# Windowed attention into a mixture of attention experts: the experts' outputs turned by DMA transposes, and some masks and casts moved to GpSimd

## The chip, the cores and the metric

The kernel runs on one core of a Trainium2 chip. The core has TensorE (PE in the profile; PEld is its weight load), VectorE (DVE), ScalarE (ACT), GpSimd (POOL) and SyncE (SP). All loads and stores are issued by SP and carried by 16 DMA engines. The metric is the time of one execution on the device in microseconds, as the median of several runs; the profile shows one such execution, from its first to its last instruction (its span).

## The reference

There are two parts. The first is attention with a sliding window over q, k and v of shape 8 batches x 8 heads x 576 rows x 64, where a row sees the rows at most 32 away. Its output, with the heads side by side, is x: 8 x 576 x 512. The second part has four attention experts over x, and a gate that picks two experts for each row:

```python
scores = np.where(np.abs(pos[:, None] - pos[None, :]) <= 32, scale * q @ k.T, -1e9)
x = softmax(scores) @ v                       # heads side by side: 8 x 576 x 512
logits = x @ w_gate                           # the two best of 4 experts, softmax of the two
for e in range(4):
    a = softmax(causal(scale * (x @ wq[e]) @ (x @ wk[e]).T))   # 576 x 576, head size 64
    out += weight_of_e_for_the_row * (a @ (x @ wv[e]) @ wo[e])
```

Inputs and outputs are float32. The kernel computes the window part with float32 matmuls and the experts with bf16 matmuls.

## The kernel before, in words

The work is cut into named steps, and a long string, `ORDER` (L22), lists them in the order in which they are emitted. Each engine executes its own instructions in that order; engines meet through semaphores. The string's entries carry the PSUM slots that a step uses after a colon: there are four slots of two banks, `P0` to `P3`, and each step that needs PSUM names its own. The `step` calls from L533 on hold the durations and dependencies that were used to lay out the order; at run time only the string matters.

The window part works on 16 groups i of four heads (two groups g per batch b):

- `load.i.qn` and `load.i.kn` (L117) bring q and k in rows as they lie in memory, 0.59 MB each; `natp` holds three buffers for each, so a load waits for the turn three groups earlier. The first two groups (`LONG`) use larger pieces.
- `turn.i.*` (L272) transposes them in blocks of 32x32 on VectorE: 2 or 6 instructions.
- `S.i.half` (L285) makes scores of 128 keys against 192 or 256 queries on TensorE, the exponential on ScalarE (three pieces for each pair of heads), and the multiplication with the band mask (L306). `MASKS` (L62) says which engine multiplies: VectorE for the groups 0 and 1, GpSimd for the other 14.
- `U.i.x` and `E.b` (`win_av` and `win_av_end`, L326 and L337) multiply with v, which `loadv.b` loads (1.18 MB) and `dup.b.n` doubles for odd blocks, on ScalarE and GpSimd; VectorE divides by the sum and writes `XN`.
- `T.b.g` and `TE.b` turn `XN` on TensorE, ScalarE copies it to `XTF` (float32) and GpSimd casts it to `XTB` (bf16).

The expert part works on batches b and pairs j of experts:

- `WL.q/v/o` load the weights and `WC.q/v/o` (L250) cast them to bf16 on ScalarE.
- `G1.b`, `G3.b`: gate. `QK.b.j.n`, `V.b.p`: projections. `PS.b.j.c`: causal scores, exponential on ScalarE, mask on GpSimd.
- `AV.b.j` (L469) multiplies with the values; VectorE scales the result by the gate's weight over the sum and writes `OE` (bf16, rows on partitions, 64 columns for each of two experts). There is one `OE` for each j, so batch b+1 overwrites that of batch b.
- `PT.b.j` (L489) turns `OE`: five TensorE transposes of 128x128 into a PSUM slot, and one VectorE copy into `OTT` (two buffers, by the parity of b).
- `Y.b.t` (L497) multiplies `OTT` with the output weights, ScalarE copies the result out of PSUM and SP stores it.

Steps `w<n>` (L216) run n matmuls on zeros to keep TensorE active while it has nothing to do, and `late.0` sets constants. SP's instructions, loads, stores and all, are one queue in program order; each transfer also waits for the one eight places before it.

Of the kernel before, what the change touches and what calls it, by code (L numbers as in the profile page):

```python
# [9 lines left out]
BF16 = mybir.dt.bfloat16  # L10
# [12 lines left out]
    load.0.qn load.0.kn load.1.kn turn.0.qn turn.0.kn load.1.qn turn.1.kn turn.1.qn loadv.0 w18:2 S.0.0:01  # L23
    w12:2 S.1.0:10 load.2.qn S.0.1:23 dup.0.0 dup.0.2 WL.q load.2.kn dup.0.3 turn.2.qn dup.0.1 S.1.1:20
    load.3.qn load.3.kn w5:1 U.1.0:3 U.0.0:2 U.1.1:0 U.0.1:3 E.0:2 turn.2.kn WC.q late.0 T.0.1:0 T.0.0:3
    turn.3.qn TE.0:2 turn.3.kn S.2.0:01 QK.0.0.0:2 WL.v S.3.0:03 QK.0.0.1:2 G1.0:1 WC.v S.2.1:20 G3.0
    QK.0.1.0:3 loadv.1 dup.1.0 V.0.0:2 dup.1.2 dup.1.3 QK.0.1.1:1 load.4.kn dup.1.1 PS.0.0.0:3 S.3.1:02
    turn.4.kn load.4.qn V.0.1:3 PS.0.0.1:1 load.5.kn turn.4.qn PS.0.1.0:0 U.3.0:3 load.6.qn U.2.0:2
    PS.0.0.2:1 S.4.0:03 load.5.qn turn.5.kn E.1:1 WL.o U.2.1:2 load.7.kn U.3.1:0 loadv.2 PS.0.0.3:1
    turn.5.qn PS.0.1.1:3 TE.1:2 T.1.0:1 T.1.1:0 PS.0.1.2:2 S.4.1:31 AV.0.0:0 QK.1.0.0:2 WC.o V.1.0:3  # L30
    PS.0.1.3:2 S.5.0:01 turn.6.qn AV.0.1:3 QK.1.1.0:2 QK.1.0.1:0 load.6.kn dup.2.1 PT.0.0:3 dup.2.0
    QK.1.1.1:2 load.8.kn PS.1.0.0:0 loadv.3 dup.2.3 S.5.1:31 dup.2.2 turn.6.kn V.1.1:2 G1.1:0 load.8.qn
    PS.1.0.1:2 G3.1 S.6.0:13 U.4.0:2 U.5.1:0 PS.1.0.2:2 load.9.qn load.7.qn dup.3.2 PS.1.1.0:1 E.2:3 U.4.1:0
    S.6.1:32 PT.0.1:0 U.5.0:1 PS.1.0.3:0 PS.1.1.1:3 load.9.kn Y.0.0:2 TE.2:1 T.2.0:0 T.2.1:3 turn.7.kn
    turn.7.qn dup.3.0 AV.1.0:1 loadv.4 turn.8.qn dup.3.1 S.7.0:02 turn.8.kn PS.1.1.2:3 V.2.0:1 QK.2.0.0:0
    Y.0.2:2 dup.3.3 PT.1.0:3 S.7.1:01 S.8.0:23 QK.2.0.1:0 G1.2:1 PS.1.1.3:0 PS.2.0.0:2 dup.4.0 U.7.1:3
    U.6.1:0 G3.2 dup.4.1 E.3:2 QK.2.1.0:3 PS.2.0.1:0 V.2.1:1 Y.0.4:2 QK.2.1.1:3 PS.2.0.2:0 load.10.kn
    turn.9.kn S.8.1:21 dup.4.3 load.10.qn U.6.0:3 U.7.0:0 PS.2.0.3:1 PS.2.1.0:2 T.3.0:3 turn.9.qn AV.1.1:0
    turn.10.kn PS.2.1.1:2 load.11.kn TE.3:1 T.3.1:3 turn.10.qn PS.2.1.2:2 load.12.qn S.9.0:01 PT.1.1:2
    dup.4.2 V.3.0:3 Y.1.0:2 AV.2.0:1 PS.2.1.3:3 QK.3.0.0:0 load.11.qn loadv.5 S.9.1:32 S.10.0:01 load.12.kn  # L40
    V.3.1:3 AV.2.1:2 Y.1.2:3 QK.3.0.1:0 PT.2.0:1 turn.11.kn turn.11.qn QK.3.1.0:2 PS.3.0.0:0 S.10.1:13
    QK.3.1.1:2 dup.5.1 PS.3.0.1:0 load.13.qn G1.3:1 PS.3.1.0:2 PS.3.0.2:0 U.9.0:3 G3.3 U.8.0:2 U.8.1:0 E.4:1
    dup.5.2 U.9.1:3 dup.5.0 PS.3.0.3:0 PS.3.1.1:2 TE.4:1 Y.1.4:0 T.4.0:3 T.4.1:1 turn.12.qn turn.12.kn
    dup.5.3 S.11.0:02 S.12.0:13 AV.3.0:0 loadv.6 QK.4.0.0:2 load.13.kn V.4.0:1 load.14.qn PS.3.1.2:2
    S.11.1:30 QK.4.0.1:1 dup.6.0 PT.2.1:2 load.15.qn G1.4:3 PS.3.1.3:2 PS.4.0.0:1 Y.2.0:0 V.4.1:2 G3.4
    turn.13.kn dup.6.1 QK.4.1.0:1 load.14.kn S.12.1:02 E.5:1 U.11.1:3 PS.4.0.1:0 QK.4.1.1:1 AV.3.1:3
    PS.4.0.2:0 PS.4.1.0:1 U.10.0:2 U.10.1:0 U.11.0:1 loadv.7 PS.4.1.1:2 PS.4.0.3:0 T.5.0:3 turn.13.qn
    PT.3.0:1 turn.14.kn TE.5:2 T.5.1:0 PS.4.1.2:3 S.13.0:21 PT.3.1:0 Y.2.2:3 turn.14.qn V.5.0:0 QK.5.0.0:1
    dup.6.3 AV.4.0:3 PS.4.1.3:0 S.13.1:12 dup.7.2 QK.5.1.0:0 QK.5.0.1:3 V.5.1:2 AV.4.1:1 dup.6.2 Y.2.4:3
    dup.7.0 QK.5.1.1:2 PS.5.0.0:0 dup.7.3 E.6:3 load.15.kn U.12.0:1 PS.5.0.1:0 PS.5.1.0:3 U.13.0:2 G1.5:1  # L50
    PS.5.0.2:2 PS.5.1.1:3 U.12.1:0 G3.5 U.13.1:2 PS.5.1.2:3 turn.15.qn T.6.0:0 Y.3.0:1 PT.4.0:3 TE.6:2
    T.6.1:0 PT.4.1:3 Y.3.2:2 PS.5.0.3:3 turn.15.kn S.14.0:10 S.15.0:32 G1.6:1 V.6.0:0 Y.3.4:2 G3.6 dup.7.1
    QK.6.0.0:3 AV.5.0:2 PS.5.1.3:1 S.15.1:30 QK.6.0.1:1 V.6.1:2 QK.6.1.0:3 PS.6.0.0:1 S.14.1:20 QK.6.1.1:3
    AV.5.1:1 PS.6.0.1:2 PS.6.1.0:3 U.15.1:0 U.14.1:2 PS.6.0.2:3 PS.6.1.1:0 E.7:1 U.15.0:2 U.14.0:1
    PS.6.1.2:0 PS.6.0.3:2 T.7.1:3 T.7.0:1 TE.7:2 PT.5.0:0 Y.4.0:3 PT.5.1:0 PS.6.1.3:1 G1.7:2 AV.6.0:1
    QK.7.0.0:3 Y.4.2:0 QK.7.0.1:3 G3.7 QK.7.1.0:1 Y.4.4:0 PS.7.0.0:3 Y.5.0:2 QK.7.1.1:0 PS.7.0.1:3 AV.6.1:1
    PS.7.1.0:0 PS.7.0.2:3 V.7.0:2 PS.7.1.1:1 Y.5.2:3 PT.6.0:0 PS.7.0.3:1 PS.7.1.2:2 V.7.1:0 PT.6.1:1 Y.5.4:3
    AV.7.0:0 PS.7.1.3:3 Y.6.0:1 AV.7.1:0 PT.7.0:3 Y.6.2:1 PT.7.1:3 Y.6.4:1 Y.7.0:3 Y.7.2:1 Y.7.4:3
# [3 lines left out]
MASKS = ["DVE"] * 2 + ["POOL"] * 14  # L62

LONG = range(2)
DUP = ["ACT", "POOL", "ACT", "POOL"]

S = 576
# [6 lines left out]
def kernel(  # L74
# [12 lines left out]
    nc = tc.nc  # L87
# [162 lines left out]
    def cast_weights(n):  # L250
        if n == "q":
            for j in range(2):
                for m in range(2):
                    nc.scalar.copy(WQK[j][m], wtmp[j][:, m, :, :])
        else:
            nc.scalar.copy({"v": WV, "o": WO}[n], wtmp[n])
# [232 lines left out]
    def moe_turn(b, j):  # L489
        OE, OTT = OES[j], OTS[b % 2]  # L490
        pt = slot("pt", BF16)[:, 0, :]
        for qt in range(NQT):
            nc.tensor.transpose(pt[:, 128 * qt:128 * qt + 128], OE[:, qt, :, :].rearrange("p e d -> p (e d)"),  # L493
                                ident_bf)
        nc.vector.tensor_copy(OTT[:, j, 0:S], pt[:, 0:S])
# [37 lines left out]
    for b in range(B):  # L533
        for g in range(2):
            i = 2 * b + g
            for nm in ("kn", "qn"):
                step(("load", i, nm), lambda b=b, g=g, nm=nm: load(b, g, nm), 0,
                     [("turn", i - 3, nm)] if i > 2 else [],
                     [("SP", 1.35, -1), ("DMA", 1.95, 0), ("LAT", 0.8, 1)] if i in LONG else
                     [("SP", 1.8, -1), ("DMA", 2.3, 0), ("LAT", 0.8, 1)])  # L540
                step(("turn", i, nm), lambda b=b, g=g, nm=nm: turn(b, g, nm), 0,
                     [("load", i, nm)] + ([("S", i - 2, 1)] if i > 1 else []),
                     [("DVE", 2.45 if i in LONG else 1.6, -1)])
            for half in range(2):
                mk = ("DVE", (0.68, 0.55)[half]) if MASKS[i] == "DVE" else ("POOL", (1.35, 1.12)[half])
                step(("S", i, half), lambda b=b, g=g, half=half: win_scores(b, g, half), (1.75, 1.1)[half],
                     [("turn", i, nm) for nm in ("kn", "qn")] + ([("S", i, 0)] if half else []) +
                     ([("U", i - 3, 0), ("U", i - 3, 1), ("E", (i - 3) // 2)] if i > 2 else []),
                     [("ACT", (1.1, 0.8)[half], -1), (*mk, 0), ("ACT", (1.1, 0.8)[half], -1), (*mk, 2)], (0, 2))
            for x in range(2):  # L550
                step(("U", i, x), lambda b=b, g=g, x=x: win_av(b, g, x), 0.98,
                     [(("S", i, h), n) for h in range(x + 1) for n in (1, 3)] +
                     [("dup", b, n) for n in range(4)] +
                     ([("T", b - 1, g)] if b else []),
                     [("DVE", 0.75, -1)], (0,))
# [7 lines left out]
        for g in range(2):  # L563
            step(("T", b, g), lambda b=b, g=g: win_turn(b, g), 0.88,
                 [("U", 2 * b + g, x) for x in range(2)] + XT,
                 [("ACT", 0.48, -1), ("POOL", 0.6, 0), ("ACT", 0.48, -1), ("POOL", 0.6, 2)], (2,))
# [5 lines left out]
        for n in range(4):  # L572
            step(("dup", b, n), lambda b=b, n=n: double_v(b, n), 0, [("loadv", b)],
                 [(DUP[n], {"ACT": 0.9, "POOL": 1.25}[DUP[n]], -1)])
        X4 = [("T", b, 0), ("T", b, 1), ("TE", b)]
        XF = [(("T", b, g), n) for g in range(2) for n in (0, 2)] + [(("TE", b), 0)]
        if b == 0:
            step(("late", 0), late_constants, 0, [], [("ACT", 0.2, -1), ("POOL", 1.2, -1)])
        if b == 0:
            for n, us in (("q", 5.8), ("v", 3.1), ("o", 1.5)):  # L580
# [3 lines left out]
                     [("ACT", {"q": 2.2, "v": 0.9, "o": 0.9}[n], -1)])  # L584
# [4 lines left out]
        for j in range(2):  # L589
# [5 lines left out]
            for c in range(4):  # L595
                step(("PS", b, j, c), lambda b=b, j=j, c=c: moe_scores(b, j, c), (0.22, 0.25, 0.24, 0.06)[c],
# [7 lines left out]
            step(("PT", b, j), lambda b=b, j=j: moe_turn(b, j), 0.3,  # L604
                 [("AV", b, j)] + ([("Y", b - 2, t) for t in (0, 2, 4)] if b > 1 else []) +
                 ([("PT", b, 0)] if j else []) + ([("late", 0)] if b == 0 else []), [("DVE", 0.4, -1)], (0,))
        for p in range(2):
            step(("V", b, p), lambda b=b, p=p: moe_proj_v(b, p), (1.75, 0.44)[p],
# [55 lines left out]
```

## Time and profile before

The kernel takes 255.18 us, the median of 3 runs (254.45 to 255.73). The profiled execution took 254.34 us, with a span of 252.6 us and a mean granted TensorE clock of 0.993.

| Engine | busy us of 252.6 | share |
|---|---|---|
| PE | 236.0 | 93% |
| ACT | 190.5 | 75% |
| PEld | 183.5 | 73% |
| DVE | 167.6 | 66% |
| POOL | 147.2 | 58% |

The DMA engines moved 40.49 MB, at 160 GB/s on the mean. Busy times are averages over a span whose parts have different limits: the row of DMA shares and a table of busy time by stretches tell more than the totals. A group's row in the profile reads: line, engine, operation, written tile <- read tiles, shape, count | busy us, mean ns of one | idle time of the engine just before, and what ended it.

The work that the change touches:

| What | where | count | mean ns |
|---|---|---|---|
| transposes of OE | TensorE L493 | 80 | 219 |
| copies to OTT | VectorE L495 | 16 | 450 |
| masks of groups 0 and 1, half 0 / half 1 | VectorE L306 | 4 / 4 | 976 / 689 |
| masks of the other groups, half 0 / half 1 | GpSimd L306 | 28 / 28 | 1545 / 1277 |
| casts of q and k weights | ScalarE L254 | 4 | 617 to 620 |
| warm-up matmuls | TensorE L219 | 35 | 506 |

### The profile page before, as it was taken

Reading aid. Unit: us, or ns where it says so; the run is one execution under the profiler, and the core shown is the slowest. Engines: PE = TensorE matmul, PEld = TensorE weight load, DVE = VectorE, ACT = ScalarE, POOL = GpSimd, SP = SyncE. Lnnn points to the kernel's source line nnn. Section 1 sums busy time; section 2 is a strip of 40 time slices with the busy share of each in tenths; the row PEclk is TensorE's granted clock in tenths of the full one; section 3 lists DMA queues with packets and bytes.
Section 4 is the critical chain, followed back from the end, with each engine's and each line's share of the span. In section 5 each row is a group of like instructions: output and inputs, shape, how many; then the busy total and the mean of one; then the engine's idle time right before and its main releaser. Section 6 shows DMA issues by size and latency. Waiting matters only on the chain. (4 is left out here: it accounts for less than half of the span.)

```text
span 252.6 us, 9868 instructions
## 1 busy us (share of the span) xinstructions
PE 236.0 (93%) x4115; PEld 183.5 (73%) x4115; DVE 167.6 (66%) x480; ACT 190.5 (75%) x372; POOL 147.2 (58%) x200
## 2 busy tenths in 40 slices
PE   7787999899999989999999999999999999999982
PEld 2455867678878878788877877898777877976640
DVE  6968954785776693788388826896568364653552
ACT  2169579969789978789889689678878868657842
POOL 6033078849596769668577499359607677350410
PEclk9997999999999999999999999999999999999999
DMA  6999999999999993069599499655140310024247
GB/s 179 300 200 202 216 163 221 209 212 207 208 205 216 238 247 117 3 169 213 153 200 262 97 223 213 186 103 121 53 118 32 139 23 3 3 86 148 112 155 253
DMA packets 74780, 40.49 MB, mean 160 GB/s; under 512 B 46832, under 2 KB 69872, under 8 KB 74736
## 3 DMA queue, kind: packets, MB, share of 16 engines
q1 hardware_dynamic: 74736, 39.87, 70.6%
q8 instruction: 32, 0.52, 0.9%
q14 instruction: 12, 0.10, 0.2%
HBM read 30.42 MB, written 9.44 MB: 158 GB/s over the span
## 5 line engine op out<-in xcount | busy, mean ns | idle before, releaser
L306 POOL TENSOR_TENSOR AT<-AT,MASKP 128x640 f32<-128x640 f32 (+1 forms) x56 | 77.6, 1411 | 28.4 <-ACT AT L303 26.1
L303 ACT ACTIVATE AT<-sc 128x384 f32<-128x384 f32 (+4 forms) x192 | 70.5, 393 | 20.9 <-PE sc L296 19.2
L455 ACT ACTIVATE ATE<-ps 128x1024 bf16<-128x1024 f32 (+1 forms) x64 | 51.9, 834 | 13.5 <-PE ps L452 12.9
L296 PE MATMUL sc<-Tqn,KT 32*128 32x192 f32 (+1 forms) x1280 | 55.3, 314 | 5.9 <-ACT AT L303 2.8
L296 PEld LDWEIGHTS sc<-Tqn,KT 32*128 32x128 f32 x1280 | 48.0, 187 | 12.0 <-ACT AT L303 4.1
L459 POOL TENSOR_SCALAR_AFFINE_SELECT ATE<-ATE 128x384 bf16<-128x384 bf16 x32 | 16.0, 524 | 32.6 <-ACT ATE L455 31.4
L326 PE MATMUL u<-VS,AT 128*64 128x65 f32 x1024 | 33.5, 223 | 0.8 <-issue 0.8
L326 PEld LDWEIGHTS u<-VS,AT 128*64 128x64 f32 x1024 | 31.5, 138 | 3.7 <-issue 2.3
L316 DVE TENSOR_TENSOR XN<-u,rs 128x512 f32<-128x512 f32 (+1 forms) x40 | 25.5, 638 | 1.4
L282 DVE STREAM_TRANSPOSE Tqn<-qn 128x192 f32<-128x192 f32 x84 | 25.1, 400 | 1.8 <-DMA qn<-in_q_dram 1.8
L282 DVE STREAM_TRANSPOSE KT<-kn 128x192 f32<-128x192 f32 x84 | 25.1, 400 | 1.4 <-DMA kn<-in_k_dram 1.4
L426 DVE CAST QKE<-pp 128x576 bf16<-128x576 f32 x16 | 12.1, 754 | 20.5 <-PE pp L419 20.5
L352 POOL CAST XTB<-XTF 128x512 bf16<-128x512 f32 x32 | 18.5, 615 | 11.2 <-ACT XTF L351 11.1
L151 POOL COPY VS<-VS 64x1024 f32<-64x1024 f32 x16 | 16.6, 1035 | 12.3 <-DMA VS<-in_v_dram 11.7
L503 PE MATMUL py<-WO,OTT 128*128 128x512 bf16 x80 | 20.9, 379 | 1.2 <-DVE ysb L517 0.6
L509 ACT COPY ysb<-py 128x1024 f32<-128x1024 f32 (+1 forms) x21 | 18.2, 868 | 4.1 <-PE py L503 3.3
L435 PE MATMUL pv<-WV,XTB 128*128 128x256 bf16 x160 | 20.1, 273 | 0.6 <-ACT ATE L455 0.3
L452 PE MATMUL ps<-QKE 64*128 64x64 bf16 (+4 forms) x192 | 19.2, 279 | 0.6 <-ACT ATE L455 0.5
L351 ACT COPY XTF<-tx 128x512 f32<-128x512 f32 x32 | 16.7, 599 | 3.3 <-PE tx L348 3.2
L435 PEld LDWEIGHTS <-XTB 128*128 128x128 bf16 x160 | 15.1, 98 | 4.6 <-issue 1.8
L419 PE MATMUL pp<-XTB,WK 128*128 128x288 bf16 x128 | 18.4, 286 | 0.0
L419 PE MATMUL pp<-XTB,WQ 128*128 128x288 bf16 x128 | 18.4, 286 | 0.0
(81 smaller groups left out, 310.7 us busy)
## 6 DMA issues: line engine op xcount, KB each, us to landing
qn<-in_q_dram SPq DMA_DIRECT2D x56, 144.0 KB, 5.1
kn<-in_k_dram SPq DMA_DIRECT2D x56, 144.0 KB, 4.9
out_dram<-ysb SPq DMA_DIRECT2D x14, 512.0 KB, 2.8
VS<-in_v_dram SPq DMA_DIRECT2D x24, 256.0 KB, 5.5
VS<-in_v_dram SPq DMA_DIRECT2D x16, 192.0 KB, 5.1
qn<-in_q_dram SPq DMA_DIRECT2D x6, 192.0 KB, 4.2
kn<-in_k_dram SPq DMA_DIRECT2D x6, 192.0 KB, 4.3
out_dram<-ysb SPq DMA_DIRECT2D x8, 128.0 KB, 2.3
```

The source lines that it names most:

```text
L282: nc.vector.transpose(T[:, dh, :].rearrange("q (a p s) -> q s a p", p=32, s=3)[:, x], n_[:, x:18:3, d])
L296: nc.tensor.matmul(sl[hh // 2][:, hh % 2, at:at + hi - lo], KT[r, dh, 128 * m:128 * m + 128], QT[r, dh, lo:hi], start=(dh == 0), stop=(dh ...
L303: nc.scalar.activation(ab[p0:p1, :, slice(*o), :], sb[p0:p1, :, slice(*i), :], EXP, scale=scale_att)
L306: eng.tensor_tensor(out=ap, in0=ap, in1=MASK[:, None, c0:c1].to_broadcast([128, 2, c1 - c0]), op=MULT)
L316: nc.vector.tensor_tensor(out=o, in0=u[:, :, :, 0:64], in1=rs[:, :, :, None].to_broadcast([128, n, 4, 64]), op=MULT)
L326: nc.tensor.matmul(us[64 * y:64 * y + 64, t, 65 * hh:65 * hh + 65], A[:, hh, 64 * a:64 * a + 64], V[:, a, 4 * g + hh, 0:65], start=True, s ...
L352: nc.gpsimd.tensor_copy(XTB[:, 2 * g + y, 0:512], XTF[:, 2 * g + y, 0:512])
L419: nc.tensor.matmul(pp[:, half, 0:HS], WQK[j][n][:, dt, :], XTB[:, dt, HS * half:HS * half + HS], start=(dt == 0), stop=(dt == NDT - 1))
L435: nc.tensor.matmul(o, XTB[:, dt, 128 * t:128 * t + 128], WV[:, dt, :], start=(dt == 0), stop=(dt == NDT - 1))
L452: nc.tensor.matmul(ps[:, eo, at:at + hi - lo], QKE[r, 1, 128 * kt:128 * kt + 128], QKE[r, 0, lo:hi], start=True, stop=True)
L455: nc.scalar.activation(ATE[0:rows, :, 512 * c:512 * c + w], ps[0:rows, :, 0:w], EXP, scale=scale_moe)
L503: nc.tensor.matmul(py[:, t - t0, :], OTT[:, j, 128 * t:128 * t + 128], WO[:, j, :], start=(j == 0), stop=(j == 1))
```

## The change

For batches 0 to 6, `PT.b.j` becomes one DMA transpose on SP's queue, from `OE` to `OTT`; it uses neither TensorE, nor VectorE, nor a PSUM slot. Batch 7 keeps the old way. The masks of group 0 (the first four heads of batch 0) move from VectorE to GpSimd, and the four casts of the q and k weights from ScalarE to GpSimd. The durations given to the steps are changed, and the order string is a new one throughout: the same steps in another sequence, with other PSUM slots. The warm-up matmuls are now 18, 9, 9, 6, 2 and 1 (45) where they were 18, 12 and 5 (35).

```diff
-    load.0.qn load.0.kn load.1.kn turn.0.qn turn.0.kn load.1.qn turn.1.kn turn.1.qn loadv.0 w18:2 S.0.0:01
-    w12:2 S.1.0:10 load.2.qn S.0.1:23 dup.0.0 dup.0.2 WL.q load.2.kn dup.0.3 turn.2.qn dup.0.1 S.1.1:20
...
+    load.0.qn load.0.kn load.1.qn load.1.kn turn.0.qn turn.0.kn loadv.0 turn.1.qn load.2.qn load.2.kn
+    turn.1.kn late.0 WL.q w18:2 S.0.0:01 dup.0.1 dup.0.3 w9:3 S.1.0:02 S.0.1:13 turn.2.qn load.3.qn WC.q
+    dup.0.2 dup.0.0 w9:0 S.1.1:12 w6:0 U.0.0:3 U.0.1:1 U.1.0:2 U.1.1:0 E.0:3 T.0.0:1 load.3.kn w2:2 TE.0:3
...
+    dup.3.3 load.7.qn load.9.qn G3.1 S.6.0:12 QK.1.1.1:0 V.1.1:3 dup.3.1 U.5.1:1 turn.7.qn load.7.kn
+    turn.7.kn PS.1.0.3:3 PS.1.1.0:0 T.2.0:2 T.2.1:1 S.6.1:03 PT.0.0 E.2:2 AV.0.1:1 PS.1.1.1:2 TE.2:0
+    AV.1.0:3 turn.8.qn PS.1.1.2:2 S.7.0:01 turn.8.kn V.2.0:3 WL.o dup.3.0 PS.1.1.3:0 loadv.4 WC.o G1.2:2
...
+    PS.7.0.2:2 V.7.0:1 PT.6.1 PS.7.1.1:0 Y.5.2:2 V.7.1:1 PS.7.0.3:0 PS.7.1.2:3 Y.5.4:2 AV.7.0:0 PS.7.1.3:2
+    Y.6.0:3 AV.7.1:0 PT.7.0:2 Y.6.2:3 PT.7.1:2 Y.6.4:3 Y.7.0:2 Y.7.2:3 Y.7.4:2
...
-MASKS = ["DVE"] * 2 + ["POOL"] * 14
+MASKS = ["POOL", "DVE"] + ["POOL"] * 14
...
-                    nc.scalar.copy(WQK[j][m], wtmp[j][:, m, :, :])
+                    nc.gpsimd.tensor_copy(WQK[j][m], wtmp[j][:, m, :, :])
...
     def moe_turn(b, j):
         OE, OTT = OES[j], OTS[b % 2]
-        pt = slot("pt", BF16)[:, 0, :]
-        for qt in range(NQT):
-            nc.tensor.transpose(pt[:, 128 * qt:128 * qt + 128], OE[:, qt, :, :].rearrange("p e d -> p (e d)"),
-                                ident_bf)
-        nc.vector.tensor_copy(OTT[:, j, 0:S], pt[:, 0:S])
+        if b == B - 1:
+            pt = slot("pt", BF16)[:, 0, :]
+            ...
+            nc.vector.tensor_copy(OTT[:, j, 0:S], pt[:, 0:S])
+            return
+        nc.sync.dma_start_transpose(OTT[:, j, :].rearrange("p (t c) -> p t c", c=128),
+                                    OE[:, :, :, :].rearrange("p t e d -> p (t e d)"))
```

## The prediction

> **What bounds the kernel now.** I read the page's first two parts, then the table of busy time by stretches, then TensorE's timeline step by step, then who waited for whom.
>
> ```profile
> span 252.6 us, 9868 instructions
> PE 236.0 (93%) x4115; PEld 183.5 (73%) x4115; DVE 167.6 (66%) x480; ACT 190.5 (75%) x372; POOL 147.2 (58%) x200
> ...
> DMA  6999999999999993069599499655140310024247
> ```
>
> The stretches (columns: PE, PEld, DVE, ACT, POOL busy with counts, clock, DMA share, GB/s):
>
> ```profile
> 60.00:78.00 18.00, 17.92 (x343) 14.68 (x343) 11.40 (x36) 15.14 (x32) 13.35 (x16) 1.00 1.17 203
> 78.00:95.00 17.00, 16.08 (x303) 13.38 (x300) 13.27 (x40) 14.99 (x30) 12.49 (x16) 1.00 1.06 236
> 95.00:107.00 12.00, 11.73 (x233) 9.12 (x232) 6.33 (x21) 9.73 (x21) 10.44 (x11) 1.00 0.18 59
> 107.00:130.00 23.00, 23.00 (x418) 18.93 (x417) 15.79 (x46) 19.92 (x41) 17.18 (x22) 1.00 0.82 180
> 200.00:230.00 30.00, 29.58 (x500) 23.36 (x493) 16.76 (x51) 20.73 (x44) 17.44 (x23) 1.00 0.11 37
> ```
>
> Two regimes are to be seen. Up to 95 us the DMA engines never rest (share 1 or more), TensorE is full as well, and loads arrive just in time. From 95 us on the DMA share falls to 0.18, later to 0.11, while TensorE stays at 98 to 100%: there TensorE alone sets the pace, and no other engine passes 87%.
>
> The just-in-time arrival is visible in two places, VectorE's timeline and TensorE's (after "x": count; in brackets the idle time before and its releaser):
>
> ```profile
> 88.08 1.80 DVE L282 STREAM_TRANSPOSE Tqn<-qn 128x192 f32<-128x192 f32 x6 [0.97 <-DMA qn<-in_q_dram]
> ...
> 20.39 2.16 PE L296 MATMUL sc<-Tqn,KT 32*128 32x192 f32 x32 [2.45 <-ACT AT L303]
> 22.48 2.09 PE L219 MATMUL warm<-WARM 128*128 128x512 bf16 x5
> 24.50 3.95 PE L326 MATMUL u<-VS,AT 128*64 128x65 f32 x128
> ...
> 236.63 0.44 PE L493 MATMUL pt<-ident_bf,OE 128*128 128x128 bf16 x5
> ```
>
> The rows that the change touches:
>
> ```profile
> L493 PE MATMUL pt<-ident_bf,OE 128*128 128x128 bf16 x80 | 7.1, 219 | 0.7 <-DVE OTT L495 0.7
> L495 DVE COPY OTT<-pt 128x576 bf16<-128x576 bf16 x16 | 7.2, 450 | 6.1 <-PE pt L493 6.1
> L254 ACT CAST WQ<-tmpw 128x512 bf16<-128x512 f32 x2 | 1.2, 620 | 0.0
> L352 POOL CAST XTB<-XTF 128x512 bf16<-128x512 f32 x32 | 18.5, 615 | 11.2 <-ACT XTF L351 11.1
> L306 POOL TENSOR_TENSOR AT<-AT,MASKP 128x640 f32<-128x640 f32 x28 | 42.6, 1545 | 14.0 <-ACT AT L303 11.8 <-issue 2.2
> L306 DVE TENSOR_TENSOR AT<-AT,MASKP 128x640 f32<-128x640 f32 x4 | 3.7, 976 | 2.0 <-ACT AT L303 1.9
> out_dram<-ysb SPq DMA_DIRECT2D x8, 128.0 KB, 2.3
> ```
>
> **What the Trainium skill says.** "VectorE: DVE Perf Modes", section "The three transpose paths", gives 1309 ns for a 128x128 bf16 DMA transpose and 390 ns on TensorE. Pipelined, the trace is far below the latter: five transposes occupy 0.28 us from the first start to the next step. "DMA: Bandwidth & Descriptors", section "Latency and other measured facts", gives 261 GB/s for a DMA transpose; the trace before has none. The same page, section "Queues, rings and completion order", says that everything SP issues shares one row of rings: the page's part 3 agrees, with all 39.87 MB of the kernel's transfers on q1. So a transpose queues with the loads.
>
> **The change, part by part.**
>
> *Transposes leave TensorE.* Read start to start in TensorE's timeline, a PT step (five matmuls) takes 0.28 us undisturbed: 14 x 0.28 = 3.9 us. The real gaps of those 14 steps add up to 4.65 us, because some wait for something else; I count 3.9. Two of the 14 lie before 89 us (at 69.9 and 82.8 us), in the regime where DMA also binds; twelve lie later: 3.4 us on the path.
>
> *Copies leave VectorE.* 14 x 0.45 = 6.3 us. VectorE is 66% busy, so I count none of it. Each PT also gives back one of four PSUM slots for some 0.7 us; too little to count.
>
> *Transposes arrive on SP.* 14 more issues beside some 200. A 128 KB store costs 0.47 us of SP and lands in 2.3 us; a transpose moves 160 KB. Lower bound: 2.3 us. Upper: five tiles in sequence at the page's price, 5 x 1.31 = 6.5 us (an estimate). I take 3, and 5 while loads are queued (their median is 5). Slack, from TensorE's step durations in the new order: between the end of AV.b.1's matmuls and Y.b.0 lie 30.7, 15.3, 9.5, 23.1, 16.6, 16.7 and 6.2 us for b = 0 to 6. VectorE's scaling (0.23 + 0.17 + 0.88 us plus gaps) takes 1.4 of that. Only b = 6 is tight: 4.8 us for 0.5 of issue and 3 of transfer, on idle rings: hidden; at 6.5 it would stall about 2.2 us. Behind each waiting PT on SP stand loads and stores, and behind these the turns on VectorE. The loads of q and k that follow are mostly placed 10 to 45 us of TensorE time ahead of their scores, so waits of 2 to 4 us are absorbed.
>
> The scaling of AV.b+1.j now waits for PT.b.j to have landed, since it overwrites OE. The tightest is PT.0.0 before AV.1.0, 2.1 us apart in TensorE time; VectorE reaches that scaling near 89.5 us by the sums below, while PT.0.0 is issued right behind the last load of k for group 7 and should land within 1 to 4 us of it, by 89.5: free, but barely.
>
> *Casts to GpSimd.* 4 x 0.615 = 2.5 us there (from the XTB row) and 4 x 0.62 - overlap = 2.1 us less on ACT. GpSimd's timeline is empty from 21.6 to 31.4 us; QK.0 starts at 33.8. Nothing on the path.
>
> *Masks.* Group 0 costs GpSimd 2 x 1.55 + 2 x 1.28 = 5.7 us in place of 3.3 on VectorE. In order: memsets move into the idle time before 15 us; masks 14.9 to 18.0; v's two copies (2.1 us) to 20.1; masks of half 1 to 22.9; casts to 25.4. U.0 starts near 24: not late. VectorE still finishes group 1's last mask near 26.1, as before, but U.0.0 now goes first, so the U steps need not wait.
>
> *Warm-ups.* 45 matmuls instead of 35, at 0.23 us 2.3 us more. Nine stand in the 2.45 us of idle time shown at 20.39, and three more stand where S.2 and S.3 wait for loads anyway: S.3.0 began at 36.0 us because its k landed at 34.2, and the new SP order still has 6.9 MB up to that load. Head: no gain, no loss.
>
> *The DMA-bound stretch.* Group 7's scores start at 89.2 us, after 18.0 MB of loads (19 of 0.59, four of v of 1.18, weights 2.1), landed at 88.1: 0.205 MB per us. The new order makes k the last load for group 7, at 17.5 MB: 85.5 us. But VectorE meets its turn earlier (by TensorE's sums near 78), and behind that turn stand the scalings of E.2, AV.0.1 and AV.1.0; TensorE waits for E.2 at TE.2. Turn to 87.3, scaling 0.6, then TE.2, AV.1.0 and a PS (1.5 us of TensorE): group 7 at about 89.4, level with before, with 0.6 us of other work still undone. Sum: 3.4 gained later, 0.6 lost here; some of the remaining waits (start to start, TensorE's steps exceed the lower quartile of their kind by about 20 us in all) belong to PT copies, +0.6. Net 3.4: span 249.2. The median of the runs, 255.18, stands 2.6 above the profiled span (that run itself measured 254.34), so I forecast 251.6 us, 1.4% faster.
>
> **Rivals.**
> A. *The new order also waits less* (0.15). Its planning durations lie nearer to the trace (turns 1.75, six rows of some 0.295; exponentials 1.3, rows adding up to 1.32; before 1.6 and 1.1). If a fifth of the 20 us of excess goes, span 245 to 246: 247.5 us. Against: TensorE is already at 98 to 100% from 107 us on.
> B. *The gain is eaten* (0.15). In the DMA-bound stretch k for group 7 lands 2 us later than reckoned, or the transposes of batches 0 and 1 hold VectorE through OE: 254.5 us. For: 2.1 us of slack at PT.0.0, and VectorE's order there. Against: loads only need to keep the rate they had.
> C. *Slower: each transpose holds the shared rings* (0.12). At 6.5 us each with the rings blocked, the seven transposes between about 85 and 165 us take 45 us. Free ring time there is 0.82 x 12 us plus some 0.15 x 53: 18 us. It decides at 2.6 us of blocking each; beyond it loads slip by up to 27 us, leads of 15 to 37 us absorb about 20, and the rest returns as 7 us against the 3.4 gained: 259 us. Against: 160 KB is small beside 0.59 MB loads.
>
> **Numbers.** Forecast 0.58, its own range 249.5 to 253.7; A 0.15, B 0.15, C 0.12. Faster by over 0.5% (about what a measurement here can tell from no change, so under 253.9) holds the forecast, A and a third of B: 0.78; within: 0.09; slower: C and the rest of B: 0.13. The range reaches from within A to the near side of C: 247.0 to 257.5.
>
> **What would show it.** Right: five of TensorE's matmuls per turn gone in 14 places; transposes landing in 2 to 5 us; Y.6.0 not waiting for one; group 7's scores still near 89 us and the gain appearing after it, at about 0.3 us per PT; DMA share up to 95 us unchanged. Wrong: TensorE idle before Y with a DMA as releaser; VectorE waiting for a DMA at the OE scaling; loads landing well over 5 us beside a transpose; a DMA share near 1 after 107 us; or TensorE's idle time between 107 and 230 us (1.3 us before: 123 us less 121.72 busy) grown to several us by the new order.

## The result and the profile after

The changed kernel takes 251.62 us, the median of 4 runs (251.29 to 252.06), beside 255.01 us for the kernel before (4 runs, 254.45 to 255.73). The ratio is 0.9867, with a 95% interval of 0.9837 to 0.9896: 1.3% faster, where 251.6 us had been forecast. Run once more later, beside another set of runs of the kernel before, it took 251.67 us, at a ratio of 0.9809 (0.976 to 0.9858); this second set has a profile of its own, called the second profile below. Medians here are of all runs, while ratios and their intervals are of those runs alone that were in the faster of the two states that executions show, so that a ratio need not be that of the medians. The profiled execution of the kernel after has a span of 249.8 us (252.6 before) at a mean clock of 0.991 (0.993 before).

The page of the kernel after (parts 1 to 3: busy time of each engine, DMA share in 40 slices, and the queue of SP with packets, MB and share of the 16 DMA engines):

```profile
PE 233.2 (93%) x4037; PEld 180.8 (72%) x4055; DVE 162.0 (65%) x462; ACT 189.0 (76%) x371; POOL 155.6 (62%) x208
...
DMA  6999999999999999999448999857453325123456
...
q1 hardware_dynamic: 84144, 42.16, 79.9%
```

TensorE lost 2.8 us of busy time, as much as the span (4.2 us in the second profile, whose span of 249.0 us is 3.6 shorter). VectorE lost 5.6 and GpSimd gained 8.4; neither number is to be seen in the time. The row of DMA shares stays near full for longer. From 60 to 95 us it is 1.10 and 1.11, about as before. The stretches behind that show where it changed (columns: stretch, length, PE, PEld, DVE, ACT, POOL busy with counts, clock, DMA share, GB/s):

```profile
95.00:107.00 12.00, 12.00 (x222) 9.53 (x220) 6.36 (x22) 10.75 (x22) 8.16 (x7) 1.00 1.00 194
107.00:130.00 23.00, 22.66 (x432) 18.68 (x431) 16.16 (x47) 19.08 (x40) 18.82 (x23) 1.00 0.89 162
200.00:230.00 30.00, 29.46 (x516) 22.86 (x518) 15.10 (x49) 22.36 (x41) 14.39 (x21) 1.00 0.28 80
```

From 95 to 107 us the DMA engines are now as full as before that (1.00; it was 0.18), and from 200 to 230 us their share is 0.28 instead of 0.11. TensorE does not notice: 12.00 of 12.00 us busy, and 29.46 of 30.

The tile `OTT` (least, median and longest duration of SP's part in ns; then the time from issue to landing in us):

```profile
L498 SPq DMA_TRANSPOSE OTT<-OE x14: 1199/1284/2692, 81.2 to 231.7; - x14
...
DMA to landing us min/median/max: 2.6/4.3/6.3
```

TensorE's timeline of the kernel after, at five places: the head, group 7's scores (L296), the outputs (L507) of batches 2 and 6, and the last matmuls:

```profile
23.11 2.60 PE L219 MATMUL warm<-WARM 128*128 128x512 bf16 x6 [1.89 <-ACT wsink L220]
25.64 4.41 PE L326 MATMUL u<-VS,AT 128*64 128x65 f32 x128
...
87.78 0.39 PE L452 MATMUL ps<-QKE 64*128 64x448 bf16 x4 [1.42 <-DVE XN L316]
...
89.71 2.03 PE L296 MATMUL sc<-Tqn,KT 32*128 32x128 f32 x48
...
151.03 1.46 PE L507 MATMUL py<-WO,OTT 128*128 128x512 bf16 x5
...
236.75 0.82 PE L507 MATMUL py<-WO,OTT 128*128 128x512 bf16 x3
...
244.54 0.59 PE L507 MATMUL py<-WO,OTT 128*128 128x512 bf16 x2 [0.64 <-DVE ysb L521]
```

Group 7's scores and the last matmuls before:

```profile
89.22 0.50 PE L296 MATMUL sc<-Tqn,KT 32*128 32x128 f32 x8 [0.47 <-ACT XTF L351]
...
247.80 0.59 PE L503 MATMUL py<-WO,OTT 128*128 128x512 bf16 x2 [0.58 <-DVE ysb L517]
```

The lines of batches 2 and 6 have no bracket: these outputs did not wait for their transposes. The closest of all is batch 2, whose second transpose SP issued with loads queued:

```profile
144.27 1.94 SPq L498 DMA_TRANSPOSE OTT<-OE  x1
```

It landed 5.9 us later, at 150.2, and the first weight load that needs it started at 151.46: 1.3 us to spare (1.2 in the second profile). At batch 6, where the transpose was issued at 231.68, it is 2.4 us. (The line at 151.03 begins with the last output of batch 1.)

Group 7's scores begin at 89.71 us (89.22 before), behind a wait of 1.42 us for VectorE, whose timeline says why:

```profile
85.45 1.79 DVE L282 STREAM_TRANSPOSE KT<-kn 128x192 f32<-128x192 f32 x6 [1.49 <-DMA kn<-in_k_dram]
...
90.02 0.88 DVE L485 TENSOR_TENSOR OE<-po,rg 128x512 bf16<-128x512 f32 x2
```

The turn of k waited 1.49 us for its load, and the scaling of `XN` that TensorE needed stood behind it. The scaling into `OE` at 90.02 us is that of AV.1.0, which overwrites what the first transpose reads; it shows no wait for a DMA, as that transpose had landed at 86.1 us.

The last matmuls of the kernel start at 247.80 us before and at 244.54 after, 3.3 us earlier. As group 7's scores start 0.5 us later than before, 3.8 us were gained between the two, and 4.4 if the 0.6 us of other work is counted that now stands behind those scores. About 0.5 was given back behind the last matmul, where ScalarE's last copy now ends a chain through a store of 2.42 us.

### The profile page after: what moved, and what is told of

It reads as the page before. It is cut to its first block, busy times and chain, and to the rows that moved or that the text cites. A ratio compares the mean times of both kernels' runs of the same rounds, so it can differ in the third digit from the quotient of the medians.

```text
span 249.8 us, 9770 instructions
## 1 busy us (share of the span) xinstructions
PE 233.2 (93%) x4037; PEld 180.8 (72%) x4055; DVE 162.0 (65%) x462; ACT 189.0 (76%) x371; POOL 155.6 (62%) x208
## 3 DMA queue, kind: packets, MB, share of 16 engines
q1 hardware_dynamic: 84144, 42.16, 79.9%
## 4 chain that ended last, share of the span: by engine, by line
PE 58%; DMA 15%; DVE 11%; SPq 6%; ACT 5%; issue 3%; ACTq 0%; DVEq 0%
PE sc L296 14%; PE pp L419 10%; DMA qn<-in_q_dram 8%; PE pv L435 6%; PE po L476 5%; PE u L326 5%; PE py L507 5%; PE tx L348 4%; PE ps L452 4%; DMA kn<-in_k_dram 3%; DVE XN L316 3%; DMA VS<-in_v_dram 3%; PE pg L378 2%; SPq L127 2%; ACT AT L303 2%
## 5 line engine op out<-in xcount | busy, mean ns | idle before, releaser
L306 POOL TENSOR_TENSOR AT<-AT,MASKP 128x640 f32<-128x640 f32 (+1 forms) x60 | 83.1, 1410 | 37.2 <-ACT AT L303 27.7
L296 PE MATMUL sc<-Tqn,KT 32*128 32x192 f32 (+1 forms) x1280 | 55.1, 311 | 2.2 <-DVE KT L279 1.9
L296 PEld LDWEIGHTS sc<-Tqn,KT 32*128 32x128 f32 x1280 | 48.1, 185 | 8.9 <-issue 2.7
L326 PEld LDWEIGHTS u<-VS,AT 128*64 128x64 f32 x1024 | 32.2, 139 | 4.2 <-issue 2.0
L326 PE MATMUL u<-VS,AT 128*64 128x65 f32 x1024 | 34.8, 225 | 0.1
L351 ACT COPY XTF<-tx 128x512 f32<-128x512 f32 x32 | 16.9, 597 | 8.0 <-PE tx L348 7.7
L438 DVE CAST VE<-pv 128x1024 bf16<-128x1024 f32 x8 | 9.8, 1220 | 19.6 <-PE pv L435 19.6
L507 PE MATMUL py<-WO,OTT 128*128 128x512 bf16 x65 | 18.7, 379 | 1.5 <-DVE ysb L521 0.6
L476 PEld LDWEIGHTS <-ATE 128*128 128x128 bf16 x480 | 16.5, 97 | 2.6 <-POOL ATE L466 0.8
```

Of the source, the lines that this page charges most:

```text
L296: nc.tensor.matmul(sl[hh // 2][:, hh % 2, at:at + hi - lo], KT[r, dh, 128 * m:128 * m + 128], QT[r, dh, lo:hi], start=(dh == 0), stop=(dh ...
L306: eng.tensor_tensor(out=ap, in0=ap, in1=MASK[:, None, c0:c1].to_broadcast([128, 2, c1 - c0]), op=MULT)
L326: nc.tensor.matmul(us[64 * y:64 * y + 64, t, 65 * hh:65 * hh + 65], A[:, hh, 64 * a:64 * a + 64], V[:, a, 4 * g + hh, 0:65], start=True, s ...
L476: nc.tensor.matmul(po[:, eo, 65 * qt:65 * qt + 65], ATE[:, eo, o:o + 128], VE[:, kt, 2 * j + eo, :], start=(kt == 0), stop=(kt == qt))
L507: nc.tensor.matmul(py[:, t - t0, :], OTT[:, j, 128 * t:128 * t + 128], WO[:, j, :], start=(j == 0), stop=(j == 1))
```

## The experiments

In most of the expectations Theory 1 is the one of the prediction: the gain is TensorE's time for fourteen turns, and the transposes, the masks and the casts are hidden. Its rivals give the gain to the new order or to the head, or say that the transposes cost time through the DMA rings. Where an experiment moves loads or takes away warm-ups, the theories are about that place alone. Each ratio is to the kernel before, with its 95% interval. In the cuts of the order string, "..." stands for steps left out.

### Turns back on TensorE, in the new order

```diff
-        if b == B - 1:
-            pt = slot("pt", BF16)[:, 0, :]
...
-        nc.sync.dma_start_transpose(OTT[:, j, :].rearrange("p (t c) -> p t c", c=128),
+        pt = slot("pt", BF16)[:, 0, :]
...
-    ... S.6.1:03 PT.0.0 E.2:2 ...
+    ... PT.0.0:2 S.6.1:03 E.2:2 ...
```

All sixteen turns are transposes on TensorE again, each in the PSUM slot that had been free longest; thirteen of the fourteen steps moved by a few places for that.

> The changed kernel with its new order, its masks and casts, but all 16 PT steps on TensorE and VectorE again, each given the PSUM slot that is longest free at its place (places moved by a few steps). Theory 1, the gain is TensorE time taken off a full TensorE: 14 x 0.28 = 3.9 us come back, plus 0 to 1.5 us for slot waits: 255.0 to 257 us, at or a little above the kernel before (255.0). Theory 2, the gain is the new order (with masks and casts on GpSimd) and not the transposes: 251.5 to 252.5 us.

Measured: 266.3 us (runs from 262.84 to 267.27), ratio 1.0383 (1.032 to 1.0447), span 264.8 us. This is some 9 us above the most that Theory 1 allowed, and further from Theory 2. TensorE's waits in this kernel (who waited for whom: us in all, times, longest), and then its timeline at one place:

```profile
PE pt L493 <- ACT AT L303: 4.2, 6, 1.3
```

```profile
89.44 1.06 PE L337 MATMUL u<-VS,AT 128*64 128x65 f32 x16 [2.30 <-DVE OTT L495]
```

The turns waited for PSUM slots that ScalarE was still emptying; and the copy to `OTT`, queued on VectorE behind a turn that waited for a DMA, held a slot for which TensorE waited 2.30 us. TensorE's idle time between 107 and 230 us is 4.0 us, against 1.4 in the kernel after. So a turn on TensorE in this order costs about 1 us (14.7 us over fourteen by the medians, 13 by the ratios). The span is 15.0 us longer than that of the kernel after: TensorE is idle for 7.7 us more and busy for 7.3 more. The turns are 3.9 of these; the rest is the same work taking longer, as behind the wait of 2.30 us, where the 30 matmuls of an `AV` step took 1.83 us, and those of the next one, less than 3 us later, 1.08. The new order has no room for the turns in the slots I chose; a better layout of them was not tried. This run therefore doesn't measure the 0.28 us of TensorE alone; the one with idle matmuls, below, does.

### The transposes alone, in the old order

```diff
-    ... PT.0.0:3 dup.2.0 QK.1.1.1:2 ...
+    ... PT.0.0 dup.2.0 QK.1.1.1:2 ...
```

The kernel before with the change's `moe_turn`; the fourteen `PT` steps keep their places and lose their slots.

> The kernel before, with only the PT steps of batches 0 to 6 made DMA transposes; order, masks, casts and warm-ups as before. Theory 1: the 3.9 us are gained here too, less what TensorE waits for transposes that the old order places close to their Y: Y.1.0 comes 5.9 us and Y.6.0 6.8 us of TensorE time after its AV, of which scaling (1.4), issue (1.3) and a landing of 2.6 to 6.3 us take all or more: 0 to 3 us lost: 251.5 to 254.5 us. Theory 2, the order makes the gain: 255 us or more.

Measured: 270.77 us, ratio 1.0588 (1.0534 to 1.0642), span 269.5 us, 16 us slower than the kernel before and as far from what Theory 1 expected. The waits of TensorE's weight loads for transposes in it, and SP's timeline around the first output:

```profile
PEld L507 <- DMA OTT<-OE: 15.0, 5, 5.7
```

```profile
76.09 9.40 SPq L127 DMA_DIRECT2D qn<-in_q_dram  x12
85.59 1.22 SPq L498 DMA_TRANSPOSE OTT<-OE  x1
```

TensorE's outputs wait 15.0 us for transposes, in five waits (the matmuls behind these weight loads are idle in the same time, which is not to be added). TensorE's idle time in whole is 31.7 us against 16.6 before, 15.1 more, which is most of the 16.9 us by which the span grew. `OE` of the transpose issued at 85.59 was complete at 69.3 us (a scaling of 0.88 us that began at 68.40); the transpose stood 16 us in SP's queue, behind a load of v and three of q that SP took 14.6 us to issue while the rings were full (DMA share 1.18 to 1.23). The landing is not slow, 3.8 us in the median: the place in the queue is. In the kernel after the first transpose stands 15 us in the queue too, but its output comes 33 us after it has landed. So the transposes are free only where the order leaves room for SP's queue, and the order of the change is part of its effect.

### Masks and casts back

```diff
-MASKS = ["POOL", "DVE"] + ["POOL"] * 14
+MASKS = ["DVE"] * 2 + ["POOL"] * 14
...
-                    nc.gpsimd.tensor_copy(WQK[j][m], wtmp[j][:, m, :, :])
+                    nc.scalar.copy(WQK[j][m], wtmp[j][:, m, :, :])
```

> The changed kernel with the masks of group 0 back on VectorE and the q, k casts back on ScalarE; order and DMA transposes as changed. Theory 1: both lie beside other work in the head, where S.3 waits for its load until 36 us: 251.6 us, within 0.7. Theory 2, that part of the gain comes from the move: 253 us or more.

Measured: 257.84 us, ratio 1.0108 (1.0073 to 1.0143): a miss by 6 us. TensorE's timeline in the head of this kernel:

```profile
31.10 2.72 PE L219 MATMUL warm<-WARM 128*128 128x512 bf16 x6 [9.52 <-ACT wsink L220]
33.74 2.44 PE L326 MATMUL u<-VS,AT 128*64 128x65 f32 x76
```

In the new order `WC.q` stands early. On ScalarE its first cast sat 2.94 us waiting for a weight, with the copy that ends a warm-up (`wsink`) and copies of v behind it; TensorE stood idle for 9.5 us, and U.0 began at 33.74 instead of 25.64. The 8.1 us lost there had shrunk to 4.9 at the end (by the spans, 254.7 and 249.8). So two readings were left: the casts belong on GpSimd, or they only may not stand at this place in ScalarE's queue.

### Masks and casts back, casts later

```diff
-    ... turn.2.qn load.3.qn WC.q dup.0.2 dup.0.0 ...
+    ... turn.2.qn load.3.qn dup.0.2 dup.0.0 ...
...
-    ... E.0:3 T.0.0:1 ...
+    ... E.0:3 WC.q T.0.0:1 ...
```

The kernel of the experiment before, with this step alone moved.

> As e3 (masks of group 0 on VectorE, q and k casts on ScalarE), but with the cast step moved to after E.0, as it stood in the old order: in e3 ScalarE waited from 21 to 28 us for weights ahead of copies of v that the first U needs. Theory 1, the moves of masks and casts are worth nothing by themselves, and e3 lost its time to the place in ScalarE's queue alone: 251.6 us, within 0.8. Theory 2: the mask of group 0 on VectorE or the casts on ScalarE cost the head 1 us or more, which is not made up by 36 us: 252.5 to 254 us.

Measured: 252.27 us, ratio 0.9875 (0.984 to 0.9911), span 249.7 us, level with the change. Moving masks and casts is worth nothing by itself that the times show. What it buys is that `WC.q` may stand early, where on ScalarE urgent copies stood behind it.

### k of group 7 one load earlier

```diff
-    ... load.7.qn load.9.qn G3.1 ...
+    ... load.7.qn load.7.kn G3.1 ...
...
-    ... turn.7.qn load.7.kn turn.7.kn ...
+    ... turn.7.qn load.9.qn turn.7.kn ...
```

> The changed kernel with two loads exchanged on SP: k of group 7 before q of group 9. In the changed kernel's trace VectorE waits 1.49 us for that k, and TensorE 1.42 us for VectorE behind it. Theory 1, the stretch up to 95 us is paced by the order of bytes: the wait goes and 1.0 to 1.5 us are gained, 250.1 to 250.6 us. Theory 2: TensorE meets the next late load instead (group 8's or v's), and it is 251.3 to 251.8 us.

Measured: 251.11 us, ratio 0.9861 (0.9811 to 0.991), span 249.0 us. The wait of 1.42 us before group 7's scores is gone from TensorE's timeline, and the scores start at 88.89, 0.8 us earlier than in the kernel after. But in the second profile of the kernel after itself, where that wait is there (1.40 us), they start at 89.11 and the span is 249.0 too. The median lies between what the two theories expected. One load earlier is worth no more than 0.2 us in the traces, and nothing that the times show.

### TensorE's time alone

```diff
+        if n == 1 and b < B - 1:
+            for _ in range(5):
+                nc.tensor.matmul(pp[:, 0, HS:HS + 128], WARM[:, 0:128], WARM[:, 0:128],
+                                 start=True, stop=True, skip_group_check=True)
```

The kernel after, with five matmuls of 128x128 on zeros at the start of the steps `QK.b.j.1` of the batches 0 to 6: fourteen times five, as many as the turns had. They wait for nothing of their own, stand in unused columns of that step's slot, and nobody reads them.

> The changed kernel with five matmuls of 128x128 bf16 on zeros added ahead of each QK.b.j.1 of batches 0 to 6, into unused columns of that step's PSUM slot: the time that the five transposes of a PT step took on TensorE, 14 times over, with no wait, slot or copy of its own. Theory 1, TensorE's time is the path: 14 x 0.28 = 3.9 us more, less what the two or three in the stretch before 90 us cost nothing: 254.6 to 255.6 us. Theory 3, what the PT steps cost was their waits (slot, VectorE copy), not their time: under 253 us.

Measured: 255.55 us (22 runs), ratio 1.0047 (1.0024 to 1.0071). By the medians this is 3.9 us above the kernel after, 0.28 us each, and by the ratios 4.6. It gives back the whole gain, with nothing else undone, and a little more: with that time put back the kernel is 0.2 to 0.7% slower than the kernel before. This is the run that carries the explanation, though it adds TensorE's time where the change took it away. Its trace has the stretch from group 7's scores to the last matmuls:

```profile
91.58 2.03 PE L296 MATMUL sc<-Tqn,KT 32*128 32x128 f32 x48
...
250.22 0.59 PE L511 MATMUL py<-WO,OTT 128*128 128x512 bf16 x2 [0.63 <-DVE ysb L525]
```

From the start of the five to the next matmul are 0.28 to 0.29 us (99.80 to 100.09 for one set). The stretch holds ten of the fourteen sets and takes 158.6 us, against 154.8 in the kernel after: 0.38 us for each. What exceeds 0.29 is mostly waiting (TensorE's idle time between 107 and 230 us is 2.2 us, against 1.4).

### Each transpose twice

```diff
+    OT2 = consts.tile([128, 640], BF16, name="OTX")
...
+        nc.sync.dma_start_transpose(OT2[:, :].rearrange("p (t c) -> p t c", c=128),
+                                    OE[:, :, :, :].rearrange("p t e d -> p (t e d)"))
```

The kernel after; the second transpose goes into a tile that nobody reads.

> The changed kernel with each of the 14 DMA transposes issued a second time, into a tile that nothing reads. It doubles their time on SP (1.3 us each) and on the DMA engines (from the trace: share of q1 79.9% of the span against 70.6%, so about 21 us of all rings, 1.5 each) and delays the loads and stores behind them. Theory 1, transposes lie beside TensorE's work: 251.6 to 252.6 us. Theory 2, each costs the path through the shared rings: one transpose's cost shows 14 times, 253 us or more.

Measured: 253.22 us (22 runs), ratio 0.9925 (0.9899 to 0.995): 1.6 us for fourteen more transposes, 0.11 each. By the number this is Theory 2's side (253 us or more), and the trace says how. The queue on its page, the one wait of TensorE's weight loads for a transpose, and the matmuls behind it:

```profile
q1 hardware_dynamic: 93552, 44.46, 87.6%
```

```profile
PEld L510 <- DMA OTT<-OE: 1.5, 1, 1.5
```

```profile
152.87 0.82 PE L510 MATMUL py<-WO,OTT 128*128 128x512 bf16 x3 [0.99 <-DMA OTT<-OE]
```

The packets take 220.1 us of all rings (87.6% of 251.3), 20.5 more than in the kernel after (79.9% of 249.8: 199.6); these in turn are 21.3 more than before (70.6% of 252.6: 178.3). A transpose's packets thus take about 1.5 us of all rings, both times (the second profile of the kernel after has 81.7% of 249.0, 203.4 us, which would make it 1.8 and 1.2). The one wait is at the output of batch 2, which had 1.3 us to spare in the kernel after and waits 1.5 us here; from group 7's scores to the last matmuls this kernel takes 1.1 us longer, about as much. So the cost in the trace is one turn that came too late, and not one price paid at each. Transposes are not quite free; twice as many begin to be felt. How much the first fourteen cost is not measured: none of TensorE's waits in the kernel after names one.

### Loads of group 7 ahead of those of group 8

```diff
-    ... load.6.kn load.8.qn turn.5.kn ...
+    ... load.6.kn load.7.qn turn.5.kn ...
...
-    ... PS.1.0.2:0 load.8.kn dup.3.3 load.7.qn load.9.qn ...
+    ... PS.1.0.2:0 load.7.kn dup.3.3 load.8.qn load.9.qn ...
...
-    ... turn.7.qn load.7.kn turn.7.kn ...
+    ... turn.7.qn load.8.kn turn.7.kn ...
```

> The changed kernel with the loads of q and k of group 7 exchanged with those of group 8 on SP, so that both arrive before group 8's. In e4 (k of group 7 before q of group 9) the trace won 0.82 of 1.5 us, and the chain there runs through the load of k for group 6 and TensorE. Theory 1: waits at group 7 go, 250.6 to 251.0 us, limited by the same load of group 6. Theory 2: group 8's k, now 1.2 MB later, becomes the late one at 95 us: 251.5 us or more.

Measured: 250.37 us, ratio 0.9824 (0.9784 to 0.9863), span 247.9 us. TensorE's timeline there:

```profile
88.02 2.03 PE L296 MATMUL sc<-Tqn,KT 32*128 32x128 f32 x48
```

Group 7's scores start 1.7 us earlier than in the kernel after (1.1 earlier than in its second profile), without a wait, and the chain that ended last runs through TensorE almost without a break from 38 to 98 us.

The kernel after was then run on one chip with this version:

> The changed kernel itself, beside e10 and e11 on one chip, so that they can be compared with it directly. Ratio to the kernel before 0.984 to 0.990, 251.0 to 252.2 us.

> e8 again (loads of group 7 ahead of group 8's), on the chip of e9. If waits at group 7 are what it removes, 1.0 to 1.9 us below e9 (the profiled spans differed by 1.9: 247.9 against 249.8).

Measured: 251.67 us (ratio 0.9809, 0.976 to 0.9858) for the kernel after, whose ratio lies below the range that was expected, and 250.46 (0.9788, 0.974 to 0.9837) for this version. It is the fastest of all by its medians, both times by 1.2 us; but the intervals overlap, so by the times alone that it beats the change is not shown.

### Fewer warm-ups

```diff
-    ... S.1.1:12 w6:0 U.0.0:3 ...
+    ... S.1.1:12 U.0.0:3 ...
```

The version before, also without the warm-ups of 2 and of 1.

> e8 without the last nine warm-up matmuls (w6, w2 and w1), on the first of which TensorE waits 1.9 us for a PSUM slot ahead of the first U. Theory 1: the head is paced by loads (S.3 waits for its k, V.0 for its weights until 37 us), so the first U starts 1.5 us earlier and the end does not move: within 0.4 us of e8. Theory 2: the head is paced by TensorE, and 1.5 to 2 us are gained. Theory 3: TensorE's clock falls without them, and 0.5 us or more is lost.

Measured: 250.74 us, ratio 0.9803 (0.9755 to 0.9851): no difference (0.3 us). TensorE's timeline at the scores of group 3:

```profile
36.18 0.60 PE L295 MATMUL sc<-Tqn,KT 32*128 32x128 f32 x8 [1.98 <-DVE KT L281]
36.98 3.33 PE L295 MATMUL sc<-Tqn,KT 32*128 32x128 f32 x40 [0.20 <-DVE KT L281]
```

U.0 began at 21.20, but only with two matmuls; the others waited for v until 23.00, 2.6 us before U.0 of the kernel after. The scores of group 3 still wait for their k and start at 36.18 (36.26 in the kernel after, 35.54 in the version before). What the head gains it waits away there. And after the pause 40 matmuls took 3.33 us, where 48 take 2.46 in the kernel after.

## Why the prediction was right, by its steps

- **Transposes leave TensorE: right, and shown.** The prediction priced a turn at 0.28 us and fourteen at 3.9; putting the matmuls alone back cost 3.9 us by the medians and 4.6 by the ratios. Between group 7's scores and the last matmuls 4.4 us were gained, where the sum had 3.4 for twelve turns and 0.6 of waits given back. So a turn there is worth 0.36 us, and 0.38 when it is added back: its own 0.28 and small waits around it. The versions that move only loads, masks or casts take 154.6 to 154.8 us for this stretch, as the kernel after does; what differs among them lies ahead of it.
- **The stretch bound by DMA: right.** k of group 7 landed at 85.43 us (85.5 reckoned), its scores started at 89.71 (89.4; 89.22 before). So 0.5 us was lost at their start (0.2), besides the 0.6 of work left undone there. This is the place where the order leaves something: the version with those loads earlier starts them at 88.02.
- **Copies leave VectorE, casts and masks move: no price, as said.** The run with masks and casts back, cast later, is level. But the sum treated their place as given: on ScalarE at that place the casts cost 6 us. I had named the work that hides them on GpSimd, and not asked what would be behind them on the other engine.
- **The number: closer than the sum.** The sum has 4.0 gained and 0.6 lost, net 3.4, for a span of 249.2 us; the profile has 4.4 gained, 1.1 lost at group 7 and 0.5 at the end, which the sum didn't have: net 2.8, 249.8 us (249.0 in the second profile). To get from span to time the prediction added 2.6 us. But a run takes 1.7 to 1.8 us more than its own span (254.34 and 252.6; 251.55 and 249.8); the rest came from a profiled run that was 0.8 below the median. That the two errors cancel, and 251.6 was met so closely, is luck.
- **Transposes on SP: hidden, though three terms were off.** SP's part of one takes 1.28 us in the median and up to 2.7, where the sum had 0.5, about that of a store. Landing was put at 3 to 5 us and within 2.3 to 6.5; it took 2.6 to 6.3, with 4.3 in the median, counted from the start of SP's part. At batch 6, which the prediction took for the only tight place, it saw 4.8 us of room for 0.5 + 3, and 2.7 were taken. The tightest place is batch 2, where it saw 9.5 us: the landing took 5.9 us with loads queued, and 1.3 us was left. The upper bound, taken from the Trainium skill ("VectorE: DVE Perf Modes", "The three transpose paths") as five tiles one after another at 1309 ns, held: the slowest landed in 6.3 us beside loads, but at batch 6 five tiles took 2.7.
- **U.0 near 24 us: late, without harm.** It started at 25.64. The six warm-ups ahead of it waited 1.89 us for the slot whose reader is ScalarE's `wsink`, and took 2.60 us; in the second profile of the same kernel they took 1.46, and U.0 began at 24.64. The experiment with fewer warm-ups shows that 2.6 us gained at this place reach no further than group 3's load.
- **Rival A, fewer waits: not seen.** TensorE's idle time from 107 to 230 us went from 1.3 to 1.4 us. But the prediction took the order only as a source of fewer waits, and not as a condition: with the old order and the new transposes the kernel takes 270.8 us, with the new order and turns on TensorE, in the slots tried, 266.3.
- **Rival B, the gain eaten: not seen.** k of group 7 landed as reckoned, and the scaling of AV.1.0 into `OE` began at 90.02 us, 3.9 after the first transpose had landed.
- **Rival C, held rings: not seen at this number.** It needed 2.6 us of blocking each; the packets take about 1.5. Twice as many cost 1.6 us, most of it in one wait.
- **A sign that misled.** The prediction named a DMA share near 1 after 107 us as a mark against it. The share was 1.00 up to 107 and 0.89 up to 130 us, and no wait came of it: a share says that rings are full, and only the waits say whether anyone minds.

## What to carry to other kernels

Where one engine is at 98 to 100% over a long stretch, taking work off it pays at about that work's start-to-start time (here 0.28 us, and 0.36 with the waits around it), not at the 0.22 us that the profile gives each of the five matmuls; add the same amount back as idle work on that engine, with no wait and no buffer of its own, to see whether that is all. A transfer put into a shared queue costs little by its length and much by its place: here one stood 16 us behind loads, so move it together with the order of that queue, and look for the place with the least time to spare, which need not be the one that seemed tight. The same holds for a cast: ask first what stands behind it on the engine that would otherwise do it.

## What had not been expected of the hardware

**One mask, three durations.** VectorE's mask of group 1 reads two operands from SBUF. In the head it runs beside GpSimd's copies of v and masks of group 0. GpSimd's and VectorE's timelines in the kernel after:

```profile
17.73 2.61 POOL L151 COPY VS<-VS 64x1024 f32<-64x1024 f32 x2
20.31 2.49 POOL L306 TENSOR_TENSOR AT<-AT,MASKP 128x512 f32<-128x512 f32 x2
```

```profile
17.74 1.71 DVE L306 TENSOR_TENSOR AT<-AT,MASKP 128x640 f32<-128x640 f32 x1 [3.08 <-ACT AT L303]
...
19.37 4.12 DVE L306 TENSOR_TENSOR AT<-AT,MASKP 128x640 f32<-128x640 f32 x1
```

and VectorE's in the second profile of the same kernel:

```profile
17.88 0.83 DVE L306 TENSOR_TENSOR AT<-AT,MASKP 128x640 f32<-128x640 f32 x1 [3.08 <-ACT AT L303]
```

With GpSimd 0.01 us ahead, the first mask took 1.71 us, and GpSimd's first copy 1.03; with both at the same hundredth (17.88), the mask took 0.83, the second one 1.14, and the copy 1.73. The Trainium skill ("SBUF — State Buffer", "Who interferes with whom") says that a VectorE instruction with two SBUF inputs and a GpSimd instruction that reads SBUF contend, and that the order of issue decides who blocks. The first profile agrees with it: the mask ended 0.68 us after GpSimd's copy. In the second the two starts are too close to tell who was first. The second mask of the first profile shows more: it began at 19.37 during GpSimd's second copy and ended at 23.48, 0.68 us after the last of the two masks that GpSimd ran right behind that copy. So it seems to have waited through three GpSimd instructions in a row, and not through one; what else could have held it was not tried. The version with group 7's loads earlier shows the same (1.71 and 4.11 us). Nothing waited for it here: that version began U.0 at 24.77, and the one with k one load earlier, whose masks are quick (0.83 and 1.14), at 25.64.

**Bandwidth of a transpose.** A transpose moves 160 KB, and its packets take about 1.5 us of all rings; from these two numbers some 109 GB/s are an estimate of its bandwidth. The Trainium skill ("DMA: Bandwidth & Descriptors", "Latency and other measured facts") gives 261 GB/s for a DMA transpose, measured on one kernel; the measurement decides for this place and shape (128 x 640, bf16, within SBUF).
